# K feature map in place on the PSUM bank, and the down projection's banks regrouped

## The chip, the cores and the metric

One core of a Trainium2 chip runs the kernel in one launch. A core has five engines with their own instruction queues: TensorE (PE) multiplies matrices into PSUM, VectorE (DVE) and ScalarE (ACT) do elementwise work and can read PSUM, GpSimd (POOL) does elementwise work on SBUF, and SyncE (SP) issues DMAs. PSUM has eight banks; one bank holds 128 x 512 f32 numbers. The metric is the time of one execution on the device, in microseconds (us).

## The reference

```python
x = A_x                                    # 2048 tokens x 1024, bf16
xn = layernorm(x)
q, k, v = split(xn @ wqkv)                 # 32 heads of 32
phi = lambda t: where(t > 0, t + 1, exp(t)) + 1e-6
kv = einsum("bhsd,bhse->bhde", phi(k), v)  # summed over all tokens
z = phi(k).sum(tokens)
o = (phi(q) @ kv) / (phi(q) . z + 1e-6)
s = o @ wo
g = silu((silu(xn @ w_gate) * (xn @ w_up)) @ w_down)   # hidden width 3584
out = x + s * g
```

## The kernel before

The work runs in three stages.

*Stage 1, K and V.* The 2048 tokens are 16 tiles of 128 (index `i`). A tile is normalised on DVE (`emit_stats`, `emit_rstd`, `emit_norm`), transposed on PE (tiles 0 to 7, `emit_A2`) or, for the blocks of four tiles from tile 8 on, written to `xn_dram` and read back transposed by two DMAs (`emit_A2_block`). Then `emit_B(i, c)` computes, for each of four column groups `c`, eight matmuls of 128 x 512 into one bank `kv_ps` (L397). The pool `psB` has three such banks, handed out in turn, so a bank is used again three groups later. Groups 0 and 1 are K: `emit_phi` turns the bank into the feature map. ScalarE writes `e_t` = exp (L131) and `r_t` = relu (L133), both to SBUF; DVE adds 1e-6 to `r_t` in place (L134), and a scalar_tensor_tensor (L135) writes min(e_t, 1) + r_t to `pk_sb` in bf16. Groups 2 and 3 are V, copied by ScalarE (L405). `emit_C(i)` multiplies `pk_sb` and V into three banks that accumulate over all tiles (L412); it stands on PE's queue after the first group of the next tile. At the end of the stage `emit_Q` begins; it uses the same `psB` banks and the same `emit_phi` (writing `pqT`).

During stage 1, POOL prepares the weights of stage 3: `emit_T` makes four differences of weight quarters (L207 to L210, elementwise in SBUF) and stores them to DRAM by two DMAs that it issues itself (L215).

*Stage 2* computes the remaining Q, the quotient (`emit_ND`) and `s = o @ wo` (`emit_S`), and stores `s`.

*Stage 3* goes through the tokens in two passes of 1024. For each pass, 28 products with gate and up weights (L608; seven multiplications for eight, by the sums that POOL prepared) leave `hT` in SBUF. Two banks (`zw`) of such a product lie in one tile of the pool `ppd` (two tiles of two banks), two more (`yb`, `xb`) in tiles of `pps` (four of one bank). Then `emit_down` runs twice, for 512 tokens each: four token tiles `t` with two column halves `cc`, in all eight banks, again `pps` and `ppd`. Its last part goes tile by tile: ten matmuls for a half (L685), then ScalarE's Silu from the bank (L709), two DVE operations (L710, L711) and the output DMA (L713).

In stages 1 and 2 the order on each engine is chosen by the framework's scheduler from priorities and dependences; in stage 3 PE, DVE, ACT and POOL keep the written order. SP takes its DMAs in order. Waits follow from the tiles: an instruction that writes a tile waits for the earlier readers of it.

Of the kernel before, what the change touches and what calls it, by code (L numbers as in the profile page):

```python
# [9 lines left out]
ACT = mybir.ActivationFunctionType  # L10
ALU = mybir.AluOpType
FP32 = mybir.dt.float32
# [9 lines left out]
def kernel(  # L22
# [11 lines left out]
    nc = tc.nc  # L34
    P = 128
# [9 lines left out]
    FC = F // P  # L45
# [3 lines left out]
    CW = min(512, D)  # L49
    NCC = D // CW  # L50
# [8 lines left out]
    EPS = 1e-6  # L59
# [44 lines left out]
    def xn_ap(dcs, tok):  # L104
        b = tok.start // TB
        return xn_blk_tiles[b][:, dcs, tok.start - b * TB:tok.stop - b * TB]
# [19 lines left out]
    def blk_rows_pt(t_dram, b):  # L126
        return t_dram[b * TB:(b + 1) * TB, :].rearrange("(t p) d -> p t d", p=P)

    def emit_phi(work, t_ps, dst, W):
        e_t = work.tile([P, W], FP32, name="e_t", tag="e_t")  # L130
        ex = nc.scalar.activation(out=e_t[:], in_=t_ps, func=ACT.Exp)  # L131
        r_t = work.tile([P, W], FP32, name="r_t", tag="r_t")
        nc.scalar.activation(out=r_t[:], in_=t_ps, func=ACT.Relu)  # L133
        nc.vector.tensor_scalar(out=r_t[:], in0=r_t[:], scalar1=EPS, scalar2=None, op0=ALU.add)  # L134
        nc.vector.scalar_tensor_tensor(out=dst, in0=e_t[:], scalar=1.0, in1=r_t[:],  # L135
                                       op0=ALU.min, op1=ALU.add)
        return ex

# [2 lines left out]
    phiw = p12.enter_context(tc.tile_pool(name="phiw", bufs=2))  # L141
# [3 lines left out]
    def emit_Q(b, g):  # L145
        if b not in pqT_tiles:
            pqT_tiles[b] = blk12.tile([P, G, TB], BF16, name="pqT", tag="pqT")
        pqT = pqT_tiles[b]
        btok = slice(b * TB, (b + 1) * TB)
        q_ps = psB.tile([P, TB], FP32, name="q_ps", tag="B")  # L150
        for dc in range(DC):
            nc.tensor.matmul(q_ps[:], lhsT=wq_sb[:, dc, g * P:(g + 1) * P], rhs=xn_ap(dc, btok),  # L152
                             start=(dc == 0), stop=(dc == DC - 1))
        emit_phi(phiw, q_ps[:], pqT[:, g, :], TB)
# [38 lines left out]
    def load_w_to(n):  # L193
        while w_next[0] < min(n, len(w_seq)):
            load_w()
# [45 lines left out]
    with ExitStack() as p1:  # L241
        wpool = p1.enter_context(tc.tile_pool(name="p1w", bufs=1))
        work = p1.enter_context(tc.tile_pool(name="p1work", bufs=2))
# [145 lines left out]
        def emit_B(i, c):  # L389
            tok = slice(i * P, (i + 1) * P)  # L390
            if i not in pkv_tiles:
                pk_sb = work.tile([P, D], BF16, name="pk_sb", tag="pk_sb")
                pkv_tiles[i] = (pk_sb, v_bufs[i % 2])
            pk_sb, v_sb = pkv_tiles[i]
            kv_ps = psB.tile([P, CW], FP32, name="kv_ps", tag="B")
            for dc in range(DC):
                mm = nc.tensor.matmul(kv_ps[:], lhsT=xn_ap(dc, tok), rhs=wkv_sb[:, dc, c * CW:(c + 1) * CW],  # L397
                                      start=(dc == 0), stop=(dc == DC - 1))
                if dc == 0 and c == 0:
                    marks[("B", i)] = mm  # L400
            if c < NCC:
                return emit_phi(phiw, kv_ps[:], pk_sb[:, c * CW:(c + 1) * CW], CW)
            else:
                vc = c - NCC
                return nc.scalar.copy(out=v_sb[:, vc * GPC:(vc + 1) * GPC, 0:P],  # L405
                                      in_=kv_ps[:].rearrange("p (g c) -> p g c", c=P))
# [30 lines left out]
        for i in range(NT):  # L437
            ex = emit_B(i, 0)
            if i == 0:
                gate([ex], sq_last)  # L440
            if i > 0:
                emit_C(i - 1)
            for c in range(1, NCH):
                if c == NCH // 2 and i + 2 >= TPB:
                    stats_upto(i + 7)
                emit_B(i, c)
            if i >= 2 * TPB and i % 2 == 0:
                prep(1)
            nxt = i + 2
            if nxt < NPE:  # L450
                if nxt < TPB:
                    stats_upto(nxt + 1)
                    emit_rstd(grp_of(nxt))
                elif nxt % TPB == 0:
                    stats_upto(nxt + TPB)
                    emit_rstd(grp_of(nxt))
                emit_A2(nxt)
            nb_ = (i + TPB) // TPB
            if (i + TPB) % TPB == 0 and nb_ >= PE_T_BLOCKS and nb_ < NB and i + TPB >= NPE:
                stats_upto((nb_ + 1) * TPB)  # L460
                emit_rstd(grp_of(nb_ * TPB))
                emit_A2_block(nb_)
# [11 lines left out]
    for j in range(NJ):  # L474
# [3 lines left out]
                                in1=mask[:, None, :].to_broadcast([P, ng, P]), op=ALU.mult)  # L478
        nc.vector.tensor_tensor(out=KVZ[:, g0:g0 + ng, P:P + HPG],
                                in0=kvz_ps[j][:, 0:ng, P:P + 1].to_broadcast([P, ng, HPG]),  # L480
                                in1=sel[:, None, :].to_broadcast([P, ng, HPG]), op=ALU.mult)
# [17 lines left out]
    with ExitStack() as p2:  # L499
        otp = p2.enter_context(tc.tile_pool(name="p2oT", bufs=2))  # L500
        work = p2.enter_context(tc.tile_pool(name="p2work", bufs=4))
# [94 lines left out]
    with ExitStack() as p3:  # L596
# [6 lines left out]
        def k2(shape, dt, name):  # L603
            return kp.tile(shape, dt, name=name, tag="k2")
# [62 lines left out]
        NQ = FC // 2  # L667
        NRES = 5

        def emit_down(p, sw, h, w0, last):  # L670
            ys = {}
            for t in range(TPB):
                if t < 2:
                    for c in range(NCC):
                        ys[(t, c)] = pps.tile([P, CW], FP32, name="y_ps", tag="s")[:]
                else:
                    yt = ppd.tile([P, NCC, CW], FP32, name="y_pd", tag="d")
                    for c in range(NCC):
                        ys[(t, c)] = yt[:, c, :]

            def mm(t, c, fc):
                wt = w_tiles[(p, "d%d" % sw, fc // 2)][:].rearrange("p a b -> p (a b)")
                o = (fc % 2) * D + c * CW
                tt = slice((sw * TPB + t) * P, (sw * TPB + t + 1) * P)
                nc.tensor.matmul(ys[(t, c)], lhsT=h[:, fc, tt], rhs=wt[:, o:o + CW],  # L685
                                 start=(fc == 0), stop=(fc == FC - 1), skip_group_check=True)

            for q in range(NQ - NRES):
                load_w_to(w0 + q + 6)
                for t in range(TPB):  # L690
                    for k in range(2):
                        for c in range(NCC):
                            mm(t, c, 2 * q + k)
            load_w_to(w0 + NQ)
            for t in range(TPB):
                r0 = p * TB2 + (sw * TPB + t) * P
                io = tp.tile([P, 2, D], BF16, name="io", tag="T")
                xres, s_in = io[:, 0, :], io[:, 1, :]
                nc.sync.dma_start(out=xres, in_=x2[r0:r0 + P, :])
                nc.sync.dma_start(out=s_in, in_=s_dram[r0:r0 + P, :])  # L700
                for cc in range(NCC):
                    for fc in range(2 * (NQ - NRES), FC):
                        mm(t, cc, fc)
                    nh = 2 if last and t == TPB - 1 and cc == NCC - 1 else 1
                    w_ = CW // nh
                    for hh in range(nh):
                        cs = slice(cc * CW + hh * w_, cc * CW + (hh + 1) * w_)
                        sy = k2([P, w_], FP32, "sy")
                        nc.scalar.activation(out=sy[:], in_=ys[(t, cc)][:, hh * w_:(hh + 1) * w_], func=ACT.Silu)  # L709
                        nc.vector.tensor_tensor(out=sy[:], in0=sy[:], in1=s_in[:, cs], op=ALU.mult)  # L710
                        nc.vector.tensor_tensor(out=xres[:, cs], in0=sy[:], in1=xres[:, cs], op=ALU.add)  # L711
                        eng = nc.sync if last else nc.gpsimd
                        eng.dma_start(out=out2[r0:r0 + P, cs], in_=xres[:, cs])  # L713

        with tc.manual_schedule(engines={mybir.EngineType.PE, mybir.EngineType.DVE, mybir.EngineType.Activation,
                                         mybir.EngineType.Pool}):
            base = 0
            for pi, p in enumerate(passes):
# [27 lines left out]
                base += n  # L746
                last_pass = pi == NPASS - 1
                emit_down(p, 0, h, base, False)
                base += NQ
                if not last_pass:  # L750
                    emit_Ssum(passes[pi + 1])
                emit_down(p, 1, h, base, last_pass)
                base += NQ

# [29 lines left out]
```

## Time and profile before

| | |
|---|---|
| median of 3 runs | 847.47 us (846.68 to 850.05) |
| the profiled execution | 847.79 us |
| its span, first to last instruction | 846.0 us |
| mean granted TensorE clock | 0.992 |
| busy: PE / DVE / ACT / POOL | 800.1 / 502.2 / 219.3 / 187.5 us |

A row of the profile that groups instructions reads: line, engine, operation, output<-inputs, shapes, count, busy time and mean ns of one, then the engine's idle time just before them and what ended it. A row of the timeline reads: start in us, length in us, engine, line, operation; in brackets the idle time before it and what released it. A row of waits reads: who waited for whom, us in total, times, the longest. A row by stretch reads: start and end, length, busy us and instructions of each engine, granted clock, share of the DMA engines, GB/s. Stage 1 runs to 163 us, stage 2 to about 282, the two passes of stage 3 to the end, with `emit_down` from 462 to 562 and from 741 on.

### The profile page before, as it was taken

Reading aid. Unit: us, or ns where it says so; the run is one execution under the profiler, and the core shown is the slowest. Engines: PE = TensorE matmul, PEld = TensorE weight load, DVE = VectorE, ACT = ScalarE, POOL = GpSimd, SP = SyncE. Lnnn points to the kernel's source line nnn. Section 1 sums busy time; section 2 is a strip of 40 time slices with the busy share of each in tenths; the row PEclk is TensorE's granted clock in tenths of the full one; section 3 lists DMA queues with packets and bytes.
Section 4 is the critical chain, followed back from the end, with each engine's and each line's share of the span. In section 5 each row is a group of like instructions: output and inputs, shape, how many; then the busy total and the mean of one; then the engine's idle time right before and its main releaser. Section 6 shows DMA issues by size and latency. Waiting matters only on the chain.

```text
span 846.0 us, 9994 instructions
## 1 busy us (share of the span) xinstructions
PE 800.1 (95%) x3808; PEld 432.5 (51%) x3808; DVE 502.2 (59%) x787; ACT 219.3 (26%) x344; POOL 187.5 (22%) x221
## 2 busy tenths in 40 slices
PE   5979977999999999999999999999999999999996
PEld 2434433445444666666655444456666666544442
DVE  6996499689555276676676036156676676612205
ACT  3423323455433312212212011022212212201102
POOL 0074699300111145345370010010000000000100
PEclk9999989999999999999999999999999999999999
DMA  9469988303545387876878439479877777753631
GB/s 298 167 212 334 306 297 297 127 1 101 150 137 174 112 252 233 261 250 234 262 242 278 152 126 315 137 212 341 256 236 258 257 232 259 254 176 119 224 131 50
DMA packets 149567, 178.91 MB, mean 211 GB/s; under 512 B 30736, under 2 KB 105872, under 8 KB 149520
## 3 DMA queue, kind: packets, MB, share of 16 engines
q1 hardware_dynamic: 137792, 137.25, 51.0%
q0 software_dynamic: 11584, 40.90, 13.6%
q8 instruction: 30, 0.49, 0.2%
q14 instruction: 17, 0.14, 0.0%
q10 hardware_dynamic: 144, 0.13, 0.0%
HBM read 127.93 MB, written 44.04 MB: 203 GB/s over the span
## 4 chain that ended last, share of the span: by engine, by line
PE 82%; DVE 11%; DMA 5%; ACT 1%; SPq 0%; issue 0%; ACTq 0%; DVEq 0%
PE zw L608 24%; PE y_pd L685 12%; PE y_ps L685 11%; PE xb L608 11%; PE q_ps L152 7%; PE yb L608 6%; PE s_ps L550 6%; PE kv_ps L397 4%; DVE r_t L134 3%; DVE pk_sb L135 2%; DVE stats L316 2%; DMA xn_dram<-xn_blk 2%; DMA xnT<-xn_dram 1%; DMA xp<-in_A_x_dram 1%; PE nd_ps L522 1%; DMA oT<-o_dram 1%
## 5 line engine op out<-in xcount | busy, mean ns | idle before, releaser
L685 PEld LDWEIGHTS <-hT 128*128 128x128 bf16 x896 | 87.6, 98 | 113.0 <-issue 8.4
L397 PE MATMUL kv_ps<-wkv_sb,xnT 128*128 128x512 bf16 x512 | 121.4, 395 | 2.7 <-DMA xnT<-xn_dram 1.5
L608 PE MATMUL xb<-xnT,w_sb 128*128 128x512 bf16 x448 | 115.5, 380 | 0.0
L685 PE MATMUL y_pd<-w_sb,hT 128*128 128x512 bf16 x448 | 104.5, 379 | 5.6 <-ACT sy L709 5.6
L710 DVE TENSOR_TENSOR sy<-sy,io 128x512 f32<-128x512 f32 (+1 forms) x33 | 22.3, 676 | 144.6 <-ACT sy L709 144.6
L685 PE MATMUL y_ps<-w_sb,hT 128*128 128x512 bf16 x448 | 103.5, 379 | 0.0
L608 PEld LDWEIGHTS <-w_sb 128*128 128x128 bf16 x672 | 56.8, 98 | 83.1 <-issue 30.5
L713 POOL DMA_DIRECT2D out_dram<-io x24 | 13.0, 541 | 341.1 <-DVE io L711 337.5
L397 PEld LDWEIGHTS <-xnT 128*128 128x128 bf16 x512 | 51.0, 102 | 62.9 <-issue 10.4
L134 DVE TENSOR_SCALAR r_t<-r_t 128x512 f32<-128x512 f32 x64 | 56.9, 890 | 31.3 <-ACT r_t L133 31.3
L658 ACT ACTIVATE sg<-sg 128x1536 f32<-128x1536 f32 x28 | 41.6, 1485 | 122.8 <-DVE sg L655 122.8
L550 PE MATMUL s_ps<-wo_sb,oT 128*128 128x512 bf16 x256 | 56.6, 379 | 1.5 <-DMA oT<-o_dram 1.5
L152 PE MATMUL q_ps<-xnT,wq_sb 128*128 128x512 bf16 x256 | 57.2, 379 | 0.0
L664 DVE TENSOR_TENSOR hT<-cu,sg 128x1536 bf16<-128x1536 f32 x28 | 49.9, 1782 | 0.0
L709 ACT ACTIVATE sy<-y_ps 128x512 f32<-128x512 f32 x16 | 9.6, 597 | 152.1 <-PE y_ps L685 152.1
L550 PEld LDWEIGHTS <-oT 128*128 128x128 bf16 x256 | 24.7, 98 | 30.6 <-DMA oT<-o_dram 2.0
L152 PEld LDWEIGHTS <-wq_sb 128*128 128x128 bf16 x256 | 24.6, 98 | 27.4
L135 DVE SCALAR_TENSOR_TENSOR pk_sb<-e_t,r_t 128x512 bf16<-128x512 f32 x32 | 35.8, 1118 | 1.4
L131 ACT ACTIVATE e_t<-kv_ps 128x512 f32<-128x512 f32 x32 | 19.1, 598 | 62.2 <-PE kv_ps L397 49.8
L555 POOL DMA_DIRECT2D s_dram<-s_sb x16 | 8.7, 541 | 119.2 <-ACT s_sb L552 119.2
L608 PE MATMUL zw<-S_4569,w_sb 128*128 128x512 f16 x112 | 29.0, 382 | 0.0
L608 PE MATMUL zw<-S_2652,w_sb 128*128 128x512 f16 x112 | 29.0, 382 | 0.0
(970 smaller groups left out, 1188.0 us busy)
## 6 DMA issues: line engine op xcount, KB each, us to landing
w_sb<-in_B_w_down_dram SPq DMA_DIRECT2D x56, 512.0 KB, 3.6
w_sb<-in_B_w_gate_dram SPq DMA_DIRECT2D x40, 512.0 KB, 4.7
w_sb<-in_B_w_up_dram SPq DMA_DIRECT2D x28, 512.0 KB, 5.4
o_dram<-o_blk SPq DMA_DIRECT2D x4, 1024.0 KB, 4.4
s_dram<-s_sb POOLq DMA_DIRECT2D x16, 256.0 KB, 2.6
io<-in_A_x_dram SPq DMA_DIRECT2D x16, 256.0 KB, 3.1
io<-s_dram SPq DMA_DIRECT2D x16, 256.0 KB, 3.6
xp<-in_A_x_dram SPq DMA_DIRECT2D x15, 256.0 KB, 6.2
```

Of the source, the lines that this page charges most:

```text
L131: ex = nc.scalar.activation(out=e_t[:], in_=t_ps, func=ACT.Exp)
L134: nc.vector.tensor_scalar(out=r_t[:], in0=r_t[:], scalar1=EPS, scalar2=None, op0=ALU.add)
L135: nc.vector.scalar_tensor_tensor(out=dst, in0=e_t[:], scalar=1.0, in1=r_t[:], op0=ALU.min, op1=ALU.add)
L152: nc.tensor.matmul(q_ps[:], lhsT=wq_sb[:, dc, g * P:(g + 1) * P], rhs=xn_ap(dc, btok), start=(dc == 0), stop=(dc == DC - 1))
L316: sts = [nc.vector.bn_stats(out=stats[:, c, :], in_=xr[:, c, :]) for c in range(NSC)]
L397: mm = nc.tensor.matmul(kv_ps[:], lhsT=xn_ap(dc, tok), rhs=wkv_sb[:, dc, c * CW:(c + 1) * CW], start=(dc == 0), stop=(dc == DC - 1))
L550: nc.tensor.matmul(s_ps[:], lhsT=oT[:, c, ttok], rhs=wo_sb[:, c, cc * CW:(cc + 1) * CW], start=(c == 0), stop=(c == G - 1))
L608: nc.tensor.matmul(out, lhsT=lhs(k), rhs=rhs(k), start=(first and k == 0), stop=(k == HK - 1), skip_group_check=True)
L658: nc.scalar.activation(out=c[:, 1:4, :], in_=c[:, 1:4, :], func=ACT.Silu)
L664: nc.vector.tensor_tensor(out=hv[:, TB:4 * TB], in0=c[:, 1:4, :].rearrange("p a b -> p (a b)"), in1=sg[:, 1:4, :].rearrange("p a b -> p (a ...
L685: nc.tensor.matmul(ys[(t, c)], lhsT=h[:, fc, tt], rhs=wt[:, o:o + CW], start=(fc == 0), stop=(fc == FC - 1), skip_group_check=True)
L710: nc.vector.tensor_tensor(out=sy[:], in0=sy[:], in1=s_in[:, cs], op=ALU.mult)
```

## The change

For K only, the Relu on ScalarE and the tile `r_t` go away. DVE computes max(t, 0) + 1e-6 from the bank into the same bank, and the scalar_tensor_tensor takes that bank as its second input. Q's map keeps its form. In `emit_down`, token tiles 0 and 1 now take the two-bank tiles of `ppd` and tiles 2 and 3 the single banks of `pps`; for tiles 0 and 1 both halves are computed before ScalarE reads the first.

```diff
-    def emit_phi(work, t_ps, dst, W):
+    def emit_phi(work, t_ps, dst, W, in_place=False):
         e_t = work.tile([P, W], FP32, name="e_t", tag="e_t")
         ex = nc.scalar.activation(out=e_t[:], in_=t_ps, func=ACT.Exp)
-        r_t = work.tile([P, W], FP32, name="r_t", tag="r_t")
-        nc.scalar.activation(out=r_t[:], in_=t_ps, func=ACT.Relu)
-        nc.vector.tensor_scalar(out=r_t[:], in0=r_t[:], scalar1=EPS, scalar2=None, op0=ALU.add)
-        nc.vector.scalar_tensor_tensor(out=dst, in0=e_t[:], scalar=1.0, in1=r_t[:],
+        if in_place:
+            r = t_ps
+            nc.vector.tensor_scalar(out=r, in0=t_ps, scalar1=0.0, scalar2=EPS, op0=ALU.max, op1=ALU.add)
+        else:
+            r_t = work.tile([P, W], FP32, name="r_t", tag="r_t")
+            r = r_t[:]
+            nc.scalar.activation(out=r, in_=t_ps, func=ACT.Relu)
+            nc.vector.tensor_scalar(out=r, in0=r, scalar1=EPS, scalar2=None, op0=ALU.add)
+        nc.vector.scalar_tensor_tensor(out=dst, in0=e_t[:], scalar=1.0, in1=r,
                                        op0=ALU.min, op1=ALU.add)
...
-                return emit_phi(phiw, kv_ps[:], pk_sb[:, c * CW:(c + 1) * CW], CW)
+                return emit_phi(phiw, kv_ps[:], pk_sb[:, c * CW:(c + 1) * CW], CW, in_place=True)
...
-                if t < 2:
+                if t >= 2:
                     for c in range(NCC):
                         ys[(t, c)] = pps.tile([P, CW], FP32, name="y_ps", tag="s")[:]
...
+                if t < 2:
+                    for cc in range(NCC):
+                        for fc in range(2 * (NQ - NRES), FC):
+                            mm(t, cc, fc)
                 for cc in range(NCC):
-                    for fc in range(2 * (NQ - NRES), FC):
-                        mm(t, cc, fc)
+                    if t >= 2:
+                        for fc in range(2 * (NQ - NRES), FC):
+                            mm(t, cc, fc)
```

## The prediction

> **What bounds the kernel.** I read the chain of work that ended last first, then busy time by stretches, then single instructions in the stretches where TensorE (PE) stands still.
>
> ```profile
> span 846.0 us, 9994 instructions
> ...
> PE 82%; DVE 11%; DMA 5%; ACT 1%; SPq 0%; issue 0%; ACTq 0%; DVEq 0%
> PE zw L608 24%; PE y_pd L685 12%; PE y_ps L685 11%; PE xb L608 11%; PE q_ps L152 7%; PE yb L608 6%; PE s_ps L550 6%; PE kv_ps L397 4%; DVE r_t L134 3%; DVE pk_sb L135 2%; DVE stats L316 2%; DMA xn_dram<-xn_blk 2%; DMA xnT<-xn_dram 1%; DMA xp<-in_A_x_dram 1%; PE nd_ps L522 1%; DMA oT<-o_dram 1%
> ```
>
> PE carries the end, except that VectorE (DVE) has 11% of the chain, about half of it in two lines of the feature map: L134 (the add) and L135 (min and add into `pk_sb`). Busy time by stretches shows where; the columns after the times are PE, PE's weight loads, DVE, ACT, POOL, then the granted clock.
>
> ```profile
> core 0: us, PE busy (x) PEld busy (x) DVE busy (x) ACT busy (x) POOL busy (x), PEclk, DMA share, GB/s
> 16.00:47.00 31.00, 28.09 (x171) 14.18 (x170) 30.79 (x101) 11.43 (x21) 1.96 (x2) 1.00 0.61 202
> 47.00:87.00 40.00, 31.23 (x171) 14.97 (x169) 32.33 (x54) 13.38 (x24) 27.30 (x28) 0.96 0.89 267
> ...
> 105.00:150.00 45.00, 34.75 (x162) 15.71 (x161) 43.00 (x17) 13.44 (x25) 44.78 (x50) 0.89 0.84 300
> ```
>
> From 16 to 47 DVE is full with 101 short instructions: real work. From 105 to 150 it is "busy" 43.00 us with 17 instructions. That is waiting, as the durations say (minimum/median/maximum in ns), and after them the same two lines by stretch, L134 for 16 to 47, 47 to 87 and 105 to 150, then L135 for 105 to 150:
>
> ```profile
> L134 DVE TENSOR_SCALAR r_t<-r_t x64: 377/427/5940, 16.0 to 238.3; 128x512 f32<-128x512 f32 x64
> L135 DVE SCALAR_TENSOR_TENSOR pk_sb<-e_t,r_t x32: 643/692/6278, 16.5 to 160.0; 128x512 bf16<-128x512 f32 x32
> ```
> ```profile
> 16.00:47.00 31.00, 3.33 (x8) 1.00 0.61 202
> 47.00:87.00 40.00, 6.66 (x8) 0.96 0.89 267
> ...
> 105.00:150.00 45.00, 28.04 (x9) 0.89 0.84 300
> ```
> ```profile
> 105.00:150.00 45.00, 15.37 (x8) 0.89 0.84 300
> ```
>
> Nine adds of 0.43 us would be 3.9 us; they take 28.04. Eight of L135 (STT, for scalar_tensor_tensor, from here on) at 0.69 would be 5.5; they take 15.37. So 34 us there are standing. POOL (GpSimd) tells why: in that stretch it prepares weight sums.
>
> ```profile
> 121.66 5.56 DVE L134 TENSOR_SCALAR r_t<-r_t 128x512 f32<-128x512 f32 x1 [0.30 <-ACT r_t L133]
> ```
> ```profile
> 121.34 1.16 POOL L207 TENSOR_TENSOR T_1995<-w_sb 128x512 fp32r<-128x512 bf16 x1
> ...
> 126.89 0.56 POOL L215 DMA_DIRECT2D t_g_2001<-T_1995  x1
> ```
>
> The DVE add starts while POOL is in an elementwise run and ends at 127.22, when POOL has turned to issuing a DMA. It stood through five POOL instructions. What PE loses by it:
>
> ```profile
> PE kvz_123 L412 <- DVE pk_sb L135: 10.2, 4, 4.9
> ```
> ```profile
> 87.25 1.90 PE L397 MATMUL kv_ps<-wkv_sb,xnT 128*128 128x512 bf16 x8 [1.52 <-DMA xnT<-xn_dram]
> 88.99 0.33 PE L412 MATMUL kvz_122<-v_sb_109,pk_sb 128*128 128x129 bf16 x3
> ...
> 96.36 0.34 PE L412 MATMUL kvz_122<-v_sb_108,pk_sb 128*128 128x129 bf16 x3
> ...
> 104.18 7.07 PE L397 MATMUL kv_ps<-wkv_sb,xnT 128*128 128x512 bf16 x32
> ...
> 116.84 9.75 PE L397 MATMUL kv_ps<-wkv_sb,xnT 128*128 128x512 bf16 x32
> ...
> 161.67 0.34 PE L412 MATMUL kvz_122<-v_sb_109,pk_sb 128*128 128x129 bf16 x3
> ```
>
> From 87 us on PE waits 10.2 us for `pk_sb`, and after a wait the same 32 matmuls take 9.75 us, not 7.07 (granted clock 0.89 in the stretch).
>
> **The change, part by part.**
>
> *K map, removed.* 32 ScalarE Relu:
>
> ```profile
> L133 ACT ACTIVATE r_t<-kv_ps x32: 591/592/616, 14.7 to 159.0; 128x512 f32<-128x512 f32 x32
> ```
>
>  ACT is busy 13.44 of 45 us from 105 to 150; no gain on the path by itself. The tile `r_t` is not written for K any more.
>
> *K map, the add.* It now reads and writes the PSUM bank. No row shows PSUM to PSUM. Lower bound 0.43 us (the undisturbed add), upper bound and nearest row the operations on as many f32 numbers with one PSUM operand:
>
> ```profile
> 308.58 0.69 DVE L629 TENSOR_TENSOR s_3059<-zw,s_3058 128x512 f32<-128x512 f32 x1
> ```
> ```profile
> 308.56 1.17 POOL L209 TENSOR_TENSOR T_3083<-w_sb 128x512 fp32r<-128x512 bf16 x1 [0.20 <-PE zw L608]
> ```
> ```profile
> L662 DVE TENSOR_TENSOR hT<-xb,sg x28: 680/682/682, 298.7 to 741.0; 128x512 bf16<-128x512 f32 x28
> ```
> ```profile
> L664 DVE TENSOR_TENSOR hT<-cu,sg x28: 1748/1749/2659, 299.3 to 741.6; 128x1536 bf16<-128x1536 f32 x28
> ```
>
> I take 0.69, so +0.26 each. These rows say more: L629 (one operand in PSUM, one in SBUF) takes its usual 0.69 right over a POOL elementwise instruction, and L662 (same operand places) varies by 2 ns in 28 runs, while L664 (both operands in SBUF) reaches 2659. So what stands for POOL is what reads SBUF alone: the old add and the old STT. The new add touches no SBUF, the new STT reads only `e_t` there. I take both as free of POOL: 0.69 and 0.69.
>
> *What that is worth from 87 us.* One tile of K and V goes by in 96.36 - 88.99 = 7.37 us when nothing stands. From 88.99 to the last tile's C at 161.67 are seven such periods and one shorter by C and the first group (a group is eight matmuls, 1.73, a quarter of the 7.07 less the last one's tail; three groups and C: 5.64): 57.2 us, against 72.68. Gain 15.5 us (10.2 of waiting, 5.3 of lower clock and restarts). What is late next: nothing until the bank rule below; DVE would work 4 x 0.69 = 2.8 us of each 7.37.
>
> *What the change adds.* The bank is released by the STT, no longer by the Relu. With three banks, the first K half's bank is wanted again by the fourth group, some 3.9 us after its Exp starts, the second's by the next tile's first group, 3.5 us after. Undisturbed, Exp 0.6 + add 0.69 + STT 0.69 and hand-over is 2.2: free after 87 us, where DVE does nothing else. Before that DVE is full and its order puts other work ahead:
>
> ```profile
> 49.80 0.60 ACT L131 ACTIVATE e_t<-kv_ps 128x512 f32<-128x512 f32 x1 [1.10 <-issue]
> ```
> ```profile
> 52.76 3.58 DVE L351 TENSOR_TENSOR lnw<-lnw,lna 128x4 f32<-128x4 f32 x1
> ...
> 60.29 0.68 DVE L135 SCALAR_TENSOR_TENSOR pk_sb<-e_t,r_t 128x512 bf16<-128x512 f32 x1
> ```
> ```profile
> 62.68 13.93 DMA xn_dram<-xn_blk
> ...
> 76.63 10.57 DMA xnT<-xn_dram
> ```
>
> Tile 4's second half needs 11.2 us from Exp to STT; today PE runs the next group meanwhile and waits at C, afterwards it waits before that group, which is 1.73 us worse; queued behind it on PE are all later groups and the transposes. The same may hit tile 5. DVE itself pays 8 x 0.27 = +2.2 us up to 47, and up to 87 gets back 6.66 - 8 x 0.69 = 1.1. DVE's order there leads through the normalised block to the two DMAs above and so to PE's start of tile 8 at 87.25; PE stands 1.52 us there, which covers that much of a delay on PE's side. Bounds: -3.5 (L351's 3.58 us is also a wait for POOL; shifted by 1 or 2 us it can fall into a gap), +5.7 (2.2 and two groups of 1.73). I take +1.5, the net DVE cost of 1.1 and a little of the bank wait, since most of the latter lies under the 1.52.
>
> *After K.* The Q map keeps the old form, and now starts near 146 us, when POOL still runs:
>
> ```profile
> 153.34 1.34 POOL L210 TENSOR_TENSOR T_2879<-w_sb,T_2878 128x512 fp32r<-128x512 bf16 x1
> ```
>
> Q's adds can stand until 154.7. PE has three banks, 5.2 us from 146.1, so at most 3.4 us are lost, at least none; I take 1.0, as the two `e_t` buffers let ACT empty two more banks. The Trainium skill (SBUF — State Buffer, section "SBUF: two separate sides") holds that the pair of ports shared by the two engines is locked for one instruction and the loser blocks for that long. By that Q's wait would be one POOL instruction and this term nought (828.2). The trace disagrees on the length: 5.56 us are five of them.
>
> *Down banks.* For t of 2 and 3 (before) both halves lie in one two-bank tile, and PE may not start the second half until ACT has read the first:
>
> ```profile
> PE y_pd L685 <- ACT sy L709: 5.6, 8, 0.7
> ```
>
> Eight waits (two tiles t, four calls), all on the chain. Afterwards the two-bank tiles serve t of 0 and 1, whose halves are both computed before either is read, and t of 2 and 3 have a bank each: -5.6 us. PE's order of matmuls stays. For t of 0 and 1 the first Silu comes 2.2 us later; then four DVE operations of this kind come at once:
>
> ```profile
> L710 DVE TENSOR_TENSOR sy<-sy,io 128x512 f32<-128x512 f32 (+1 forms) x33 | 22.3, 676 | 144.6 <-ACT sy L709 144.6
> ```
>
> 2.7 us, under the next t's 20 matmuls (4.3 us). The output DMAs follow in the same order on their queues, the loads of `io` stand ahead of them. Entering the stage, t = 1 now wants the last `zw`, which L655 frees:
>
> ```profile
> 461.31 1.23 DVE L655 TENSOR_TENSOR cu<-zw,s_4226 128x1024 f32<-128x1024 f32 x1 [2.22 <-PE zw L608]
> ```
> ```profile
> 461.97 2.02 PE L685 MATMUL y_ps<-w_sb,hT 128*128 128x512 bf16 x8
> ```
>
> It is free at 462.54; t = 1 starts four matmuls of 0.216 after 461.97, at 462.83. Cost nothing; without that cover some 0.3 us, four times at most.
>
> *Sum.* The profiled execution took 847.79 (span 846.0 and 1.8 around it), 0.3 above the median of 847.47. 847.8 - 15.5 + 1.5 + 1.0 - 5.6 = 829.2.
>
> **Rivals.**
> 1. *The held bank bites in every early tile.* For it: DVE is full until 47 us and the margin from Exp to STT is 3.5 to 3.9 us. Price: 0.7 us at eight halves, 5.6, beside the full 5.7: 847.8 - 15.5 - 5.6 + 5.7 + 5.6 + 1.0 = 839. The Trainium skill (VectorE: DVE Perf Modes, section "Rules for kernel authors") speaks for it: on matmul output accept the slow mode or copy to SBUF first if many operations follow. No run here shows such an exchange. Chance 0.14.
> 2. *Slower: the new STT still stands for POOL,* since it reads `e_t` and writes `pk_sb` in SBUF. Then every K half still meets a POOL run, the 15.5 stay lost, and each of the four waits after 87 us starts one group and one C earlier (2.2 us): 847.8 + 4 x 2.2 + 1.5 - 5.6 = 852.5. It decides as soon as STTs in 105 to 150 take more than about 3 us in the mean. Against it: L629 and L662. Chance 0.08.
> 3. *The gain is given back to transfers or POOL later:* stages after K then start as before, 847.8 + 1.5 - 5.6 = 843.7. Against it is PE's only DMA wait from 150 to 283 us:
>
> ```profile
> PE s_ps L550 <- DMA oT<-o_dram: 1.5, 1, 1.5
> ```
>
> Chance 0.06.
> 4. *The regrouping only moves its wait* (to the entry or to the next call): 829.2 + 5.6 = 835. Chance 0.05.
> 5. *The early stretch gains:* -3.5 in place of +1.5: 824. Chance 0.10.
>
> **How the numbers follow.** Forecast 0.57, with its own range 825 to 834. Low end: rival 5 with a Q cost of nought, 847.8 - 15.5 - 5.6 - 3.5 = 823, less 1 for PSUM operations nearer 0.43. High end: rival 1's 839. Left out: rivals 2 and 3 and a few hundredths. About 0.5% (4.2 us) is what a measurement of this kernel can tell from no change: faster 0.86 (forecast, 1, 4, 5), same 0.06 (rival 3), slower 0.08 (rival 2).
>
> **What the profile afterwards would show.** K's add at 0.65 to 0.70 us and STT at 0.69, both with maxima near their medians; no PE wait for `pk_sb` after 87 us and a clock near 1.00 in that stretch; 7.4 us per tile; Q starting near 146 to 148. The row of PE's wait for `sy` gone. A new wait of PE's `kv_ps` for `pk_sb` between 40 and 75 us, 2 to 4 us in all. I am wrong if K's STT shows times of several us, if the scheduler's order on DVE before 62 us moves the normalised block by more than 5 us, or if PE's gaps come back in Q.

## The result, and the profile after

The changed kernel takes 828.25 us (median of 4, 826.94 to 829.81) against 847.46 us, a ratio of 0.9769 [0.974, 0.9798]. The prediction's sum was 829.2. A second measurement (e9 below) gives 0.9759 [0.9717, 0.9802]. Two single runs at a granted clock of 0.57 to 0.66 (one of e3, 1185.9 us, and one of the kernel before beside e5 to e8, 1364.3 us) are left out of every comparison. The profiled execution took 827.32 us, 20.5 less than the profiled one of before (847.79); the rows below are from these two.

The page of the kernel after: span, busy time and chain.

```profile
span 825.6 us, 9966 instructions
...
PE 794.9 (96%) x3808; PEld 431.9 (52%) x3808; DVE 465.7 (56%) x787; ACT 202.9 (25%) x312; POOL 185.3 (22%) x221
...
PE 88%; DVE 8%; DMA 3%; SPq 0%; issue 0%; ACT 0%; ACTq 0%
PE zw L613 24%; PE y_pd L690 12%; PE xb L613 11%; PE y_ps L690 11%; PE kv_ps L402 9%; PE q_ps L157 7%; PE s_ps L555 6%; PE yb L613 6%; DVE stats L321 2%; DMA xp<-in_A_x_dram 1%; PE nd_ps L527 1%; DVE xn_blk L364 1%; DVE kv_ps L134 1%; DMA oT<-o_dram 1%; DMA w_sb<-in_B_w_up_dram 1%; DMA w_sb<-in_B_w_down_dram 1%
```

DVE's share of the chain fell from 11% to 8%: K's map, 3% and 2% before, is left with 1% (L134), and the weights of stage 3 appear with 1% each. By stretches (same columns as in the prediction), the kernel after:

```profile
47.00:87.00 40.00, 31.07 (x164) 15.02 (x162) 30.98 (x57) 8.88 (x15) 27.42 (x29) 0.87 0.91 285
...
105.00:150.00 45.00, 44.99 (x244) 21.82 (x243) 18.02 (x31) 14.69 (x25) 44.80 (x50) 1.00 0.88 313
150.00:163.00 13.00, 13.00 (x62) 5.89 (x61) 8.71 (x16) 8.01 (x15) 0.99 (x2) 1.00 0.20 81
```

From 105 to 150 PE is busy 44.99 of 45 us (before: 34.75), while POOL does as much as before (44.80 us, before 44.78). DVE is down from 43.00 us with 17 instructions to 18.02 with 31. From 47 to 87 nothing was gained: PE 31.07 us, before 31.23.

The instructions of the map after, minimum/median/maximum in ns. L134 is the new add, L140 the STT (`pk_sb` for K, `pqT` for Q), L139 Q's old add:

```profile
L134 DVE TENSOR_SCALAR kv_ps<-kv_ps x32: 683/700/701, 14.5 to 143.6; 128x512 f32<-128x512 f32 x32
...
L140 DVE SCALAR_TENSOR_TENSOR pk_sb<-e_t,kv_ps x32: 630/687/690, 15.7 to 144.3; 128x512 bf16<-128x512 f32 x32
...
L139 DVE TENSOR_SCALAR r_t<-r_t x32: 373/427/428, 149.9 to 222.8; 128x512 f32<-128x512 f32 x32
```

K's STT went from a maximum of 6278 ns to 690, though it still reads `e_t` and writes `pk_sb` in SBUF. C on PE (first row of tile 7, of tile 8 and of tile 15):

```profile
88.96 0.34 PE L417 MATMUL kvz_122<-v_sb_109,pk_sb 128*128 128x129 bf16 x3
...
96.33 0.34 PE L417 MATMUL kvz_122<-v_sb_108,pk_sb 128*128 128x129 bf16 x3
...
146.17 0.34 PE L417 MATMUL kvz_122<-v_sb_109,pk_sb 128*128 128x129 bf16 x3
```

Tile 7's C comes when it came (before 88.99). One tile still takes 7.37 us, and tile 15 comes at 146.17 in place of 161.67: 15.5 us. The waits of PE that differ most, first before, then after:

```profile
PE kvz_123 L412 <- DVE pk_sb L135: 16.4, 6, 5.5
...
PE kv_ps L397 <- DMA xnT<-xn_dram: 1.5, 1, 1.5
...
PE kvz_122 L412 <- DVE pk_sb L135: 1.4, 1, 1.4
```
```profile
PE kv_ps L402 <- DVE pk_sb L140: 8.9, 1, 8.9
...
PE y_pd L690 <- DMA w_sb<-in_B_w_down_dram: 1.4, 1, 1.4
...
PE xb L613 <- DMA w_sb<-in_B_w_up_dram: 0.4, 1, 0.4
```

Before, 10.2 of the 16.4 us lay behind 87 us; the other 6.2, the 1.4 and the 1.5 for the DMA, together 9.1 us, lay ahead of it. In their place there is one wait of 8.9 us for a bank that K's map still holds. The waits of `y_pd` for `sy` (5.6 us) are gone; two short ones for weights are new.

The long wait in full, from the timelines of ACT, PE, DVE and POOL of the kernel after:

```profile
55.37 0.60 ACT L131 ACTIVATE e_t<-kv_ps 128x512 f32<-128x512 f32 x1 [1.64 <-PE kv_ps L402]
```
```profile
68.12 3.57 PE L402 MATMUL kv_ps<-wkv_sb,xnT 128*128 128x512 bf16 x8 [8.93 <-DVE pk_sb L140]
```
```profile
53.70 3.99 DVE L359 TENSOR_TENSOR rstd<-rstd,lnw 128x4 f32<-128x4 f32 x1
...
57.72 3.46 DVE L364 TENSOR_SCALAR xn_blk<-xp,mv,rstd 128x1024 bf16<-128x1024 bf16 x3
...
67.38 0.69 DVE L140 SCALAR_TENSOR_TENSOR pk_sb<-e_t,kv_ps 128x512 bf16<-128x512 f32 x1
```
```profile
53.69 0.57 POOL L220 DMA_DIRECT2D t_g_912<-T_906  x1
54.27 1.17 POOL L212 TENSOR_TENSOR T_1055<-w_sb 128x512 fp32r<-128x512 bf16 x1
...
57.60 2.05 POOL L290 DMA_DIRECT2D wo_sb<-in_A_wo_dram  x2
```

ACT finished the exponential at 55.97; the STT that frees the bank ended at 68.07. DVE's list has the normalised block in between. An operation on 128 x 4 numbers stands for 3.99 us (the same line takes 0.16 at 66.18), through three POOL elementwise instructions until POOL turns to issuing DMAs. Its record starts 0.57 us ahead of the first of the three, while POOL still issues a DMA; why it did not get through in that time stays open. The first eight matmuls after the wait take 3.57 us, at a granted clock of 0.50 from 68.0 to 71.5; undisturbed, eight start every 1.73.

The down projection, by the rows where it starts and where the work after the first one starts (before, then after):

```profile
562.05 1.29 PE L608 MATMUL yb<-S_4566,T_4896 128*128 128x512 f32 x4
...
740.57 1.80 PE L685 MATMUL y_ps<-w_sb,hT 128*128 128x512 bf16 x7
```
```profile
446.53 1.67 PE L690 MATMUL y_pd<-w_sb,hT 128*128 128x512 bf16 x7
...
544.62 1.28 PE L613 MATMUL yb<-S_4502,T_4832 128*128 128x512 f32 x4
...
723.70 1.67 PE L690 MATMUL y_pd<-w_sb,hT 128*128 128x512 bf16 x7
```

The first `emit_down` pair took 100.08 us (461.97 to 562.05) and takes 98.09; the second, to the end of the span, took 105.43 and takes 101.90. Between them, pass 2's gate and up products grew from 178.52 to 179.08 us. Net: -1.99 - 3.53 + 0.56 = -4.96.

### The profile page after: what moved, and what is told of

It reads as the page before. It is cut to its first block, busy times and chain, and to the rows that moved or that the text cites. A ratio compares the mean times of both kernels' runs of the same rounds, so it can differ in the third digit from the quotient of the medians.

```text
span 825.6 us, 9966 instructions
## 1 busy us (share of the span) xinstructions
PE 794.9 (96%) x3808; PEld 431.9 (52%) x3808; DVE 465.7 (56%) x787; ACT 202.9 (25%) x312; POOL 185.3 (22%) x221
## 4 chain that ended last, share of the span: by engine, by line
PE 88%; DVE 8%; DMA 3%; SPq 0%; issue 0%; ACT 0%; ACTq 0%
PE zw L613 24%; PE y_pd L690 12%; PE xb L613 11%; PE y_ps L690 11%; PE kv_ps L402 9%; PE q_ps L157 7%; PE s_ps L555 6%; PE yb L613 6%; DVE stats L321 2%; DMA xp<-in_A_x_dram 1%; PE nd_ps L527 1%; DVE xn_blk L364 1%; DVE kv_ps L134 1%; DMA oT<-o_dram 1%; DMA w_sb<-in_B_w_up_dram 1%; DMA w_sb<-in_B_w_down_dram 1%
## 5 line engine op out<-in xcount | busy, mean ns | idle before, releaser
L402 PE MATMUL kv_ps<-wkv_sb,xnT 128*128 128x512 bf16 x512 | 117.8, 387 | 10.2 <-DVE pk_sb L140 8.9
L719 ACT ACTIVATE sy<-y_pd 128x512 f32<-128x512 f32 x16 | 8.7, 594 | 156.3 <-PE y_pd L690 156.3
L134 DVE TENSOR_SCALAR kv_ps<-kv_ps 128x512 f32<-128x512 f32 x32 | 22.3, 699 | 42.8 <-ACT e_t L131 42.7
L557 ACT CAST s_sb<-s_ps 128x512 bf16<-128x512 f32 x32 | 18.8, 586 | 38.2 <-PE s_ps L555 37.6
```

Of the source, the lines that this page charges most:

```text
L134: nc.vector.tensor_scalar(out=r, in0=t_ps, scalar1=0.0, scalar2=EPS, op0=ALU.max, op1=ALU.add)
L557: nc.scalar.copy(out=s_sb[:, cc * CW:(cc + 1) * CW], in_=s_ps[:])
```

## The experiments

My theory was the prediction's: the old add and the old STT stood because both operands were in SBUF, and each of two independent parts brings its own gain. All times are set beside runs of the kernel before on the same chip.

**e1: K's part alone.** The kernel after with `emit_down` of before.

> The K feature map changed, the down projection as before. Theory (VectorE no longer stands while GpSimd works, because K's operations read at most one operand in SBUF): all of stage 1's gain and nothing else, 847.5 - 15.5 = 832 (830 to 834); the matmuls of the down projection still wait 8 times for ScalarE, 5.6 us by the rows of waits. Rival (part of the gain in stage 1 needs the regrouped banks): impossible by the order of the stages, it would show as less than 13 us gained.

832.62 us (832.4 to 835.3), ratio 0.9821 [0.9796, 0.9845], as expected. Its waits:

```profile
PE kv_ps L402 <- DVE pk_sb L140: 8.7, 1, 8.7
...
PE y_pd L690 <- ACT sy L714: 5.6, 8, 0.7
```

The 8.7 us in the early stretch come with K's part, and the row for `sy` is back.

**e2: the down banks alone.** The kernel before with the new `emit_down`.

> The regrouping alone, the K map as before. If the row of waits gives the price (8 x 0.7 us): 847.5 - 5.6 = 841.9. If the gap between the matmuls on both sides of a wait gives it (82.57 to 83.48 in the last pass, 0.91 us, eight times): 840.2. If a transfer of down weights takes some of it back, as the 1.4 us wait in the changed kernel suggests: 841.5 to 842.5, with a wait of y_pd or y_ps for w_sb in the second call of the first pass.

844.21 us (837.83 to 847.18, 10 runs), ratio 0.9951 [0.9925, 0.9977]: a gain of about 4 us, less than I had expected. The total is a poor witness here, as its runs spread over 9 us: how POOL's runs fall on DVE in stage 1 differs from run to run (the profiled one waits 20.5 us for `pk_sb`, before 17.8, though the edit touches nothing there). The stage itself is clear in the profile of this kernel:

```profile
465.55 1.67 PE L685 MATMUL y_pd<-w_sb,hT 128*128 128x512 bf16 x7
...
562.14 1.28 PE L608 MATMUL yb<-S,T 128*128 128x512 f32 x4
...
740.68 1.67 PE L685 MATMUL y_pd<-w_sb,hT 128*128 128x512 bf16 x7
```

The first pair takes 96.59 us and the second, to the end at 842.5, 101.82: 3.49 and 3.61 less than before, 7.1 together, 0.89 for each of the eight waits (the row of waits has 0.7, which leaves out the restart). In the kernel after, 2.1 of these 7.1 are given back, most of it to the waits for weights. The profile of e2 has no such wait, though its down projection is as fast; what makes the weights late in the kernel after stays open.

**e3: the add writes SBUF.** The kernel after, but the add goes from the bank to an SBUF tile, so that the STT again has two SBUF operands and the bank is free earlier:

```diff
-            r = t_ps
+            r_t = work.tile([P, W], FP32, name="r_t", tag="r_t")
+            r = r_t[:]
```

> Changed kernel, but VectorE's max-and-add reads the bank and writes r_t in SBUF, and the scalar_tensor_tensor reads e_t and r_t, both in SBUF. ScalarE's Relu stays away, the regrouping stays in. Theory (two operands in SBUF stand for GpSimd): K's scalar_tensor_tensor again takes several us at its longest (over 4), the max-and-add stays at 0.7, tile 15 is reached 8 to 16 us later than in the changed kernel, time 836 to 843. Rival (the gain comes from one ScalarE operation and one hand-over less per half): 826 to 830, tile 15 as in the changed kernel.

843.02 us (median of 3, 840.01 to 843.79), ratio 0.9925 [0.9898, 0.9953]. The add (L135), the STT (L141) and the C of tile 15 of this kernel:

```profile
L135 DVE TENSOR_SCALAR r_t<-kv_ps x32: 671/682/692, 14.9 to 157.2; 128x512 f32<-128x512 f32 x32
```
```profile
L141 DVE SCALAR_TENSOR_TENSOR pk_sb<-e_t,r_t x32: 637/764/6022, 16.1 to 157.9; 128x512 bf16<-128x512 f32 x32
```
```profile
159.80 0.39 PE L418 MATMUL kvz<-v_sb,pk_sb 128*128 128x129 bf16 x4
```

Writing SBUF costs nothing: the add never stands. Reading two SBUF operands does: the STT reaches 6022 ns. Tile 15's C comes 13.6 us later than in the kernel after (146.17), so most of the 15.5 us gained there hang on the place of the STT's second operand. The rival, one ScalarE operation and one hand-over less, falls: the Relu is away here too, and the gain is lost all the same.

**e4: POOL held off, nothing of the change.** The kernel before; the loads that feed POOL's weight sums wait for tile 15's products.

```diff
-            load_gu(t, key[1], key[2], after)
+            hold = marks.get(("B", 15))
+            d = load_gu(t, key[1], key[2], hold)
+            if hold is None:
+                prep_loads.append(d)
...
+        gate(prep_loads, marks.get(("B", 15)), sync=True)
```

> Kernel before, but the weight loads of GpSimd's preparation wait for the first matmul of K tile 15, so that GpSimd does no elementwise work in stage 1. Only stage 1 is to be read; the work is pushed into stage 2, and the time as a whole may be worse (840 to 880). Theory: K's adds take at most 0.5 us and its scalar_tensor_tensor at most 0.75; PE has no wait for pk_sb over 1 us after 75 us, and the last C of stage 1 comes at 140 to 148 us with nothing of the change made. Rival (the map's form is what costs, GpSimd only coincides): the waits for pk_sb stay, and the last C stays near 160 us.

```profile
47.00:87.00 40.00, 40.00 (x235) 20.09 (x233) 20.69 (x59) 17.81 (x32) 1.76 (x2) 1.00 0.63 159
```
```profile
135.06 0.39 PE L418 MATMUL kvz<-v_sb,pk_sb 128*128 128x129 bf16 x4
```

With POOL idle (1.76 us) the old map does not stand: until POOL starts its sums at 132.09, no STT takes more than 0.69 us. PE is full and tile 15's C comes at 135.06, 26.6 us earlier than before and 11 earlier than after, sooner than I had expected. In one execution the kernel takes 865.91 us, because the sums then stand on Q: `q_ps` waits 15.3 us for `r_t` and `nd_ps` 20 us for DVE. So POOL is the cause of the waits in both stretches, and the change had removed only the later of them. The hold takes POOL's loads and stores away along with its sums; that the sums make the map stand is read from the durations on DVE, and from e3 against the kernel after: sums and transfers go on in both, and the STT stands only with two SBUF operands.

**e5 and e6: the cause of the 8.9 us.** e5 is the kernel after with POOL's loads held until tile 5's products, e6 the kernel after with four banks in `psB` and one in `psC` (the transposes) instead of three and two.

> Changed kernel, but GpSimd's preparation waits for the first matmul of K tile 5 (some 54 us), so that VectorE can normalise the blocks of tiles 8 to 15 alone. Theory (the 8.9 us that PE still waits in stage 1 are VectorE's normalisation standing for GpSimd, while the held bank only says where PE feels it): the wait falls under 2 us and the last C of stage 1 comes at 134 to 138 us, not 146. GpSimd then works until 155 to 165 us and Q's map, whose adds read SBUF alone, stands for it: Q loses 2 to 10 us of the 10 gained. Time 818 to 826. Rival (the bank held by the map is the cause, GpSimd is not): the wait stays above 6 us, time 827 to 831.

> Changed kernel with four banks for K, V and Q groups and one instead of two for the transposes. If the held bank is the cause of the 8.9 us: it falls to 3 us or less. If VectorE's lateness is the cause and the bank only says where PE stands: PE gets one group and a transposition further (2.2 us), waits 6 to 7 us and is done with stage 1 within 2.5 us of the changed kernel; time 826 to 829.

e5: 826.09 us (823.72 to 831.23), ratio 0.9764 [0.9701, 0.9827]. Its profile has no wait for `pk_sb`, and tile 15's C comes at 140.02, 6.2 earlier than after but later than the 134 to 138 expected; yet the total gains 2 us at most, since new waits follow (3.1 for `r_t` in Q, 2.2 for the transposing DMA), and the runs spread over 7 us. e6: 831.62 us, ratio 0.9802 [0.9754, 0.985], above the 826 to 829 expected. Its waits:

```profile
PE kv_ps L402 <- DVE pk_sb L140: 6.5, 1, 6.5
PE tr_ps L378 <- DVE xnT L379: 3.3, 3, 1.7
```

One more bank saves 2.4 of the 8.9 us and costs 3.3 at the transposes, which have one bank less; tile 15's C comes at 150.31, 4.1 later than in the kernel after. The bank says where PE feels DVE's lateness; what makes DVE late is POOL.

**e7 and e8: less that can meet POOL.** e7 is e5 with Q's map in place too. e8 (no hold) gives K and Q a map with one DVE instruction that reads one PSUM and one SBUF operand; for t > 0 it leaves out the 1e-6:

```diff
-        ex = nc.scalar.activation(out=e_t[:], in_=t_ps, func=ACT.Exp)
...
+        nc.scalar.activation(out=e_t[:], in_=t_ps, func=ACT.Relu, scale=-1.0)
+        ex = nc.scalar.activation(out=e_t[:], in_=e_t[:], func=ACT.Exp, scale=-1.0)
+        nc.vector.scalar_tensor_tensor(out=dst, in0=t_ps, scalar=EPS, in1=e_t[:],
+                                       op0=ALU.max, op1=ALU.add)
```

> As e5, and Q's map takes the bank in place too. Theory (an add in PSUM does not stand for GpSimd, wherever it is used): Q no longer loses what it lost in e5; last C at 134 to 138, Q and the rest follow without waits for the map, time 815 to 820. Rival (Q's map is covered by its buffers anyway): same time as e5 within 1 us.

> Changed kernel with another K and Q map: ScalarE computes exp(-relu(-t)) in two passes, VectorE one operation, max(t, 1e-6) plus that, one operand in PSUM and one in SBUF (for t above 0 the added 1e-6 is left out). GpSimd's work is where it was. If VectorE's amount of work counts in the full stretch from 16 to 70 us (16 halves x 0.7 us less): last C 3 to 9 us earlier, 819 to 825. If only its standing for GpSimd counts there: within 2 us of the changed kernel, 826 to 830.

Both missed. e7: 829.29 us (825.73 to 837.83), ratio 0.9796 [0.972, 0.9872]. e8: 846.33 us, ratio 0.9987 [0.9959, 1.0015], all of the gain lost. In e8's profile DVE is light, and PE waits for a transfer:

```profile
47.00:87.00 40.00, 32.27 (x178) 15.80 (x175) 17.92 (x44) 14.74 (x25) 18.65 (x20) 0.96 0.93 240
87.00:105.00 18.00, 8.84 (x38) 4.16 (x39) 1.38 (x2) 3.04 (x5) 2.63 (x3) 0.63 1.14 188
```
```profile
PE kv_ps L395 <- DMA xnT<-xn_dram: 14.5, 1, 14.5
```
```profile
66.73 30.84 SPq L383 DMA_TRANSPOSE xnT<-xn_dram  x2
```

The two transposing DMAs of stage 1, one for tiles 8 to 11 and one for 12 to 15, hold SP for 30.84 us (19.2 and 11.6), back to back and while POOL issues stores and two loads of `wo`; in the kernel after they are issued apart, 4.72 and 7.31 us long. The DMA engines are about as busy there (0.91 from 47 to 87 and 1.12 from 87 to 105, here 0.93 and 1.14), so their share does not tell why. That the freed DVE brought the two transposes and POOL's transfers together is argued, not shown. In e7's profile the second of them took 23.68 us and PE waited 8.4; it is the profile of e7's longest run (837.83). Besides, both kernels wait over 6 us for `oT` in stage 2 (after: 1.5).

**e9, e10, e11: hold the loads past the block.** e9 is the kernel after again. e10 is e7 with the hold at tile 8's products instead of tile 5's; e11 is e8 with that hold.

> The changed kernel once more, as the measure for the two below on the same chip: 827 to 830.

> Changed kernel, Q's map in place too, GpSimd's preparation held until the first matmul of K tile 8. The two transposing DMAs of stage 1 then stand ahead of all preparation loads on SP's queue. Theory (stage 1 of e7 lost 7 us because a transposing DMA stood behind preparation loads and shared the DMA engines with them, and the rest of stage 1 is free once VectorE normalises without GpSimd): no wait of kv_ps for xnT over 2 us, no wait for pk_sb over 2 us, last C at 134 to 138 us, time 815 to 820. Rival (the late start of the preparation is paid later, by the loads of stage 3 or the transposes of o behind it): last C as said, but a wait of several us for oT or w_sb before 290 us, time 820 to 830.

> e8's map (two ScalarE passes, one VectorE operation; the added 1e-6 left out for t above 0) with the preparation held until K tile 8. If e8 lost only by its transposing DMA (14.5 us of waiting for xnT, 6.2 for oT): last C at 130 to 137 us, time 812 to 820, at or below e10. If two ScalarE passes in a row are too slow for the banks: waits of kv_ps for pk_sb on every tile and more than 825.

| | median us | ratio to before | C of tile 15 | stage 3 starts |
|---|---|---|---|---|
| e9 (after) | 826.76 | 0.9759 [0.9717, 0.9802] | 146.28 | 266.75 |
| e10 | 825.81 | 0.9747 [0.9711, 0.9783] | 137.12 | 265.44 |
| e11 | 821.97 | 0.9701 [0.9665, 0.9736] | 133.97 | 260.95 |

No wait for `pk_sb` or the transposing DMA is left between 48 us and tile 15 worth naming; stage 1 gains 9 and 12 us. But stage 3 starts only 1.3 and 5.8 earlier: stage 2 gives the rest back, and both times lie above what I had expected (815 to 820 and 812 to 820). In e11's profile, on DVE and SP:

```profile
228.06 0.16 DVE L532 TENSOR_SCALAR rden<-nd_ps 128x8 f32<-128x8 f32 x1
228.13 2.28 DVE L497 TENSOR_TENSOR S<-xnT 128x2048 fp32r<-128x2048 bf16 x1
230.33 0.20 DVE L534 RECIPROCAL rden<-rden 128x8 f32<-128x8 f32 x1
230.45 2.29 DVE L498 TENSOR_TENSOR S<-S,xnT 128x2048 fp32r<-128x2048 f32 x1
232.66 0.42 DVE L535 TENSOR_TENSOR o_blk<-nd_ps,rden 128x256 bf16<-128x256 f32 x1
```
```profile
233.11 0.38 SPq L544 DMA_DIRECT2D o_dram<-o_blk  x1
```

The scheduler put two sums for stage 3 (`S`) between the steps of the last quotient, so its store is issued 6.9 us after the last ND matmul (226.23), against 2.7 in the kernel after (238.42 and 241.13). e7, e8 and e10 show the same 6.9.

**e12: the same with the sums behind the quotient.** e11, with only the first pass's `S` sums ordered after the last `o_blk`:

```diff
+        s1 = nc.vector.tensor_tensor(out=S1[:], in0=a21, in1=a22, op=ALU.add)
+        if p == passes[0]:
+            gate([s1], marks["o_last"])
...
+        s3 = nc.vector.tensor_tensor(out=S3[:], in0=a11, in1=a21, op=ALU.subtract)
+        if p == passes[0]:
+            gate([s3], marks["o_last"])
```

> The kernel of e11 (feature maps with one VectorE instruction, prep loads held until B(8)), with nothing but the order of VectorE's list changed: the S sums of the first batch (L497 to L499) stand behind the last quotient o_blk. In e11 two of these sums, 2.28 and 2.29 us, ran ahead of the last o_blk, so that o_dram was issued 6.9 us after the last ND matmul (kernel after: 2.7 us), and PE waited 6.2 us for oT (after: 1.5 us). Theory, that this order is where the held kernels lost what they gained in stage 1: the wait for oT falls to 1 to 3 us, stage 3 starts near 256 us, time 815 to 819. Rival, that the transposing DMAs of oT are late for a reason of their own (the traffic of weights behind the held loads): the wait stays near 6 us, time 820 to 824.

815.31 us (814.44 to 817.8), ratio 0.9603 [0.9581, 0.9625]: the best version, 6.7 under e11 and some 12 under the kernel after. DVE, the wait, and the start of stage 3 in its profile:

```profile
231.32 0.42 DVE L539 TENSOR_TENSOR o_blk<-nd_ps,rden 128x256 bf16<-128x256 f32 x1
231.67 2.28 DVE L497 TENSOR_TENSOR S<-xnT 128x2048 fp32r<-128x2048 bf16 x1
```
```profile
PE s_ps L559 <- DMA oT<-o_dram: 1.6, 1, 1.6
```
```profile
257.00 1.28 PE L617 MATMUL yb<-S,T 128*128 128x512 f32 x4
```

The theory holds and its rival falls: nothing was slow in the transfers, the store was issued late. The wait went from 6.2 to 1.6 us, and the mean granted clock from 228 to 256 us from 0.88 to 1.00. In the two profiles the stretch from the last ND matmul to stage 3 shrank from 34.72 us (226.23 to 260.95) to 27.93 (229.07 to 257.00), 6.8 us, as in the medians.

## Why the prediction was right

The sum was 829.2 against the profiled 827.32: a fall of 18.6 predicted, 20.5 measured.

- *K from 87 us, -15.5:* measured 15.5 (161.67 to 146.17), with the period of 7.37 us and no wait for `pk_sb`. The argument from L629 and L662 held, and e3 confirms it from the other side. The Trainium skill (SBUF — State Buffer, section "SBUF: two separate sides") counts a VectorE operation with two SBUF inputs among those that take the shared ports against a GpSimd operation that reads SBUF; e3 agrees (6022 ns with two, 690 in the kernel after with one).
- *The add at 0.69:* 0.70, about what an add from PSUM to SBUF takes (0.68 in e3).
- *The early stretch, +1.5:* measured 0.0 (tile 7's C at 88.96, before 88.99; in e1 and e9, with the same stage 1, at 89.20 and 89.08). The step mis-sized is the one for the held bank. I had expected 2 to 4 us of new wait beside what was there; it was 8.9 in one place, and it took the place of 9.1 us of old waits. Between C and the bank PE waits for the same late DVE once, not twice. That the term was off by no more than 1.5 us is in part luck: the new wait is at least twice what I expected, and the old ones that went with it made up for it.
- *Q, +1.0:* measured 0. POOL's last sums ended before the first Q add started at 149.9 (POOL works 0.99 us from 150 to 163), and Q's adds have a maximum of 428 ns. I had taken POOL's end from before (154.7); in the kernel after its last sum ends at 149.75, 4.9 us earlier, just ahead of the first Q add. So the sentence on the rule of the Trainium skill for one instruction (828.2) gives the better number for a reason that is not its own. On the length of a stand the record holds both: the early stretch again disagrees, with 3.99 us through three POOL instructions, but in POOL's last run in the kernel before, from 149.34 to 154.68, the adds and STTs of K stood through one POOL instruction each (1.37 to 1.53 us; the first is shown below the list). I had judged the rule by the long stands alone.
- *The down banks, -5.6:* measured -4.96 net. The mechanism is right and the size off in two terms: each wait costs 0.89 us, not 0.7 (e2: 7.1 in all), and 2.1 come back, as the stage reaches `w_down` and `w_up` before they have landed (1.4 and 0.4 us of waits; e2 has neither). I had looked for a new wait at the stage's entry, where there is none, and not at the weights.

```profile
149.33 1.47 DVE L134 TENSOR_SCALAR r_t<-r_t 128x512 f32<-128x512 f32 x1 [0.51 <-ACT r_t L133]
```

Of the rivals, the second (the STT still stands) falls by its maximum of 690 ns, the third (stages after K start as before) by the start of stage 3, 15.5 us earlier. The first is half there: the held bank does bite, in one early tile, for the full 8.9, but not on top of the old waits. Its page's rule, to copy matmul output to SBUF if many operations follow (the Trainium skill, VectorE: DVE Perf Modes, section "Rules for kernel authors"), would have cost some 15 us here: e3, whose add leaves its result in SBUF, takes 843.02 against 828.25. The fourth holds for 2.1 of the 7.1 us, at the weights, not at the entry or the next call. The 1.9 us by which the sum was too high are these: two costs that did not come (2.5) less 0.6 missing at the down banks.

## What to carry to other kernels

Where GpSimd does elementwise work beside VectorE, look for VectorE operations whose maximum is many times their minimum, and give them one PSUM operand: a longer instruction that never stands beats a shorter one that does. Price such a change by the time at which the next stage starts, not by the sum of waits; a wait removed early is often paid again at the next late producer (a bank, a transfer, a store behind someone else's sums). When a faster stage brings nothing, follow the first wait of the next stage back to the place of its producer in its engine's list: here two instructions in the wrong order were worth 6.7 us.

## What the runs showed of the hardware that I had not expected

- A stand of VectorE for GpSimd is not set by its own size: 3.99 us for 128 x 4 numbers (5.56 for 128 x 512 before). Both ended when GpSimd turned from elementwise work to issuing a DMA. Others let VectorE in between two elementwise instructions: the adds of 1.47 and 1.37 us at 149.33 and 152.29 before, where GpSimd's instructions start 1.20 to 1.56 us apart (1.10 to 1.12 apart in the run from 121.34 that the 5.56 us lasted through). What decides between the two stays open.
- The two transposing DMAs of stage 1, one for each block of four tiles, held SP for 30.8 us back to back among GpSimd's transfers in e8, for 17.3 back to back in e12, where the loads were held, for 12.0 apart among transfers in the kernel after, and for 8.0 apart with the loads held in e10. What is traffic and what is queueing stays open.
- After an 8.9 us wait of TensorE, the next eight matmuls took 3.57 us in place of some 1.9 (granted clock 0.50 from 68.0 to 71.5): the wait cost at least a fifth more than its length.
